# New tables of order, banks and engines for an attention and mixer kernel, with every ReLU on ScalarE

## The chip, the cores and the metric

The kernel runs on one core of a Trainium2 chip. The metric is the time of one execution in microseconds (us) on the device. A core has five engines that run side by side, each through its own instructions in a fixed order: TensorE (PE, matmuls into PSUM banks), VectorE (DVE), ScalarE (ACT), GpSimd (POOL) and SyncE (SP), which here issues all DMAs. An instruction starts when the one before it on its engine has begun to leave room and when the semaphores it waits for are set.

## The reference

Block-causal attention (8 batches, 8 heads, 576 positions, head width 64, blocks of 64), then a mixer over its output x (576 positions, 512 channels):

```
scores = scale * q @ k^T, masked by blocks;  attn = softmax(scores);  x = attn @ v
theta = x @ w_theta;  zr = x * cos(theta);  zi = x * sin(theta)
y = w_tok_r @ zr + w_tok_i @ zi          (over positions)
u = x + y
out = u + max(u @ w_ch, 0)               (w_ch over channels)
```

## The kernel before

Matmul operands are split into two float16 halves (a high part and the difference), and a product is taken as high*high + low*high + high*low, so each of the mixer's products is three matmuls. For the first three batches the scores are taken in float32 without a split.

The work is a list of 3404 parts. Per pair of heads: wide and narrow scores (`s1`, `s2`, and a small `sd`) into PSUM banks; per head the maxima of the score rows on VectorE (`m`, line 633), a bias from them (`mn`, L641, VectorE or GpSimd), the exponentials on ScalarE (`e`, L646), the cast to the high half (`high`, L431 or L433), the subtraction for the low half (`low`, L436), a transposing DMA (`turn`, tile `pt`), 45 small matmuls with v (`weighted`, L680), and the division (`normalise`, L692 to L698, tile `xn`). Per batch: x is split and turned (tiles `xp`, `xT`), theta is made (L816, L819), its turns taken off (L828 on ScalarE, L834 on VectorE), sines and cosines (L849, L851), products with x (L860, tiles `aa`, `rr`), their halves (`zh` by L431 or L433, `zl` by L436), the mix over positions (L884), x added back (L889, L893, tile `u`), halves of u (L423 to L427, L900), the channel products (L907), the ReLU (`relu`, L910 to L915), the last addition (L923) and the store. Eight batches overlap: the attention of a later batch runs beside the mixer of an earlier one. At the beginning the weights are loaded, brought to float32 (L471 to L485), scaled and split (L494 to L507) beside the attention of the first batch.

Three tables decide what the parts leave open. `ORDER` is the order in which all parts are written out; each engine runs its own parts in that order. `BANKS` gives each PSUM tile one of the eight banks, seen as `s` (banks 0 to 3) and `g` (4 to 7) in the rows. `PLACES` gives one letter to each part that may run on more than one engine (A ScalarE, D VectorE, P GpSimd). `emit` (L236) reads them:

```
        if parts[key].on:
            place[key] = next(places, parts[key].on[0])
```

The ReLU can be on ScalarE or VectorE:

```
            if on == "A":
                nc.scalar.activation(out=c, in_=c, func=AF.Relu, scale=self.scales["v"].unit)
            else:
                nc.vector.tensor_scalar(out=c, in0=c, scalar1=self.scales["v"].unit, scalar2=0.0, op0=ALU.mult, op1=ALU.max)
```

Of the kernel before, what the change touches and what calls it, by code (L numbers as in the profile page):

```python
# [37 lines left out]
    8, 9, 158, 10, 11, 160, 336, 335, 363, 364, 340, 339, 16, 17, 18, 19, 350, 341, 0, 1, 2, 3, 32, 33, 351, 334,  # L38
    361, 352, 34, 386, 24, 338, 337, 342, 25, 387, 372, 40, 41, 26, 27, 390, 392, 343, 12, 42, 35, 353, 162, 415,
    362, 365, 163, 4, 20, 414, 344, 43, 391, 56, 57, 48, 366, 373, 49, 58, 59, 374, 72, 375, 50, 51, 401, 367, 354,  # L40
    385, 164, 345, 346, 347, 44, 80, 36, 412, 413, 368, 73, 369, 74, 165, 28, 166, 64, 389, 104, 388, 393, 416, 96,
    88, 81, 355, 159, 161, 402, 52, 82, 60, 65, 97, 5, 105, 106, 13, 75, 376, 394, 403, 66, 21, 29, 89, 136, 137,
    138, 139, 348, 67, 37, 423, 424, 425, 167, 168, 169, 170, 417, 171, 45, 395, 53, 172, 76, 107, 120, 98, 99, 112,
    332, 333, 437, 396, 489, 83, 438, 349, 100, 404, 377, 405, 442, 441, 90, 370, 383, 418, 465, 84, 384, 61, 397,
    68, 69, 494, 91, 77, 466, 108, 356, 85, 92, 398, 93, 101, 141, 178, 176, 443, 357, 142, 436, 151, 474, 358, 426,
    30, 22, 359, 371, 452, 113, 143, 14, 6, 419, 114, 115, 420, 378, 440, 439, 434, 399, 121, 122, 444, 453, 379,
    463, 421, 464, 467, 445, 435, 446, 128, 15, 140, 144, 447, 540, 406, 468, 469, 454, 116, 46, 448, 470, 123, 180,
    86, 487, 427, 380, 475, 381, 31, 54, 471, 449, 490, 400, 476, 491, 360, 38, 407, 428, 514, 455, 382, 495, 496,
    408, 515, 409, 518, 410, 488, 497, 129, 493, 456, 517, 519, 130, 492, 422, 450, 457, 516, 477, 525, 429, 503,
    504, 498, 485, 505, 472, 430, 431, 478, 173, 94, 174, 152, 479, 432, 486, 131, 539, 568, 567, 526, 78, 527, 182,  # L50
    451, 506, 507, 544, 499, 543, 520, 1804, 458, 109, 538, 591, 145, 500, 1805, 411, 459, 545, 181, 508, 554, 460,
    461, 433, 541, 576, 501, 521, 528, 529, 522, 124, 70, 132, 542, 480, 566, 117, 546, 125, 133, 146, 577, 147,
    473, 481, 183, 184, 482, 39, 153, 185, 549, 483, 1807, 555, 186, 1808, 596, 556, 557, 530, 187, 509, 565, 569,
    7, 502, 188, 510, 558, 511, 512, 578, 547, 47, 579, 523, 531, 548, 550, 551, 462, 148, 580, 149, 118, 134, 126,
    189, 524, 532, 533, 484, 1806, 570, 571, 572, 534, 1810, 1811, 513, 1809, 589, 190, 150, 593, 592, 1837, 1838,
    154, 536, 587, 597, 598, 559, 535, 1813, 1812, 1823, 1814, 573, 552, 599, 1830, 23, 1831, 102, 1824, 617, 590,
    1839, 600, 616, 620, 1825, 62, 110, 537, 1832, 594, 1815, 595, 605, 588, 621, 622, 560, 606, 79, 574, 1816, 619,
    618, 71, 601, 111, 627, 607, 553, 608, 1826, 628, 1827, 561, 562, 563, 63, 1840, 1841, 1842, 1833, 609, 602,
    629, 1817, 1818, 1828, 1834, 1835, 1819, 581, 1829, 1844, 1845, 623, 1846, 1847, 1820, 1843, 1848, 575, 630,
    582, 1821, 1822, 1836, 177, 179, 610, 1849, 1850, 1851, 1852, 1860, 55, 1861, 603, 583, 638, 624, 87, 640, 103,  # L60
    584, 668, 644, 585, 667, 671, 642, 672, 625, 631, 1856, 1853, 673, 196, 641, 647, 643, 648, 649, 650, 95, 645,
    670, 646, 1864, 1854, 656, 1857, 1865, 611, 657, 604, 693, 651, 586, 194, 658, 669, 564, 1855, 678, 639, 612,
    652, 632, 1868, 1858, 698, 198, 613, 691, 614, 653, 615, 694, 1862, 692, 695, 1869, 679, 680, 659, 1859, 1870,
    654, 1866, 699, 197, 700, 701, 720, 633, 626, 634, 1908, 696, 1863, 1909, 697, 635, 1910, 1899, 1900, 1901, 660,
    1867, 661, 719, 1914, 689, 681, 690, 674, 119, 636, 199, 707, 1885, 708, 1889, 1871, 1872, 709, 721, 1911, 718,
    1902, 200, 682, 637, 1915, 1873, 675, 683, 722, 1916, 702, 703, 1912, 1881, 729, 676, 704, 705, 723, 710, 711,
    712, 1917, 1888, 655, 1880, 662, 2004, 1918, 1903, 1876, 195, 1893, 1894, 663, 1895, 1896, 664, 1907, 1919, 665,
    1892, 666, 2005, 2006, 1884, 1904, 1897, 1913, 744, 1898, 2007, 1877, 730, 731, 724, 2008, 201, 202, 203, 725,
    732, 733, 734, 684, 677, 726, 685, 1882, 1878, 743, 1879, 749, 686, 748, 687, 1886, 1890, 1874, 742, 1891, 1875,
    785, 727, 747, 745, 746, 688, 750, 751, 204, 205, 752, 706, 713, 714, 766, 715, 1944, 1945, 1883, 764, 753, 716,  # L70
    1946, 754, 755, 765, 206, 1887, 207, 1938, 767, 208, 155, 1939, 756, 156, 768, 769, 757, 135, 1940, 770, 1941,
    1947, 1948, 1942, 2010, 740, 1937, 209, 2009, 735, 1943, 771, 728, 772, 773, 781, 1949, 741, 736, 783, 737, 738,
    786, 758, 784, 789, 2023, 790, 2024, 788, 717, 826, 787, 739, 759, 791, 792, 806, 2037, 794, 1920, 1921, 795,
    796, 1905, 793, 2013, 807, 2030, 805, 808, 809, 2031, 2011, 2038, 831, 867, 797, 774, 2012, 2039, 2014, 760,
    761, 191, 2025, 192, 2032, 812, 813, 798, 127, 810, 1922, 2044, 2045, 782, 2046, 2015, 2047, 2048, 1950, 2033,
    2049, 775, 2026, 2027, 2028, 2034, 811, 2035, 157, 2040, 1906, 2041, 2042, 175, 2016, 2017, 2050, 2029, 2018,
    2019, 762, 825, 2020, 2021, 824, 1951, 2043, 2036, 799, 2022, 2051, 763, 212, 830, 829, 216, 849, 220, 2052,
    2061, 814, 815, 816, 828, 2053, 1929, 1930, 1931, 1932, 1933, 1934, 827, 776, 832, 777, 778, 833, 835, 836,
    1923, 1924, 846, 848, 1925, 1926, 847, 822, 779, 780, 1927, 800, 1952, 834, 823, 1928, 1935, 850, 1958, 1959,
    1994, 1936, 1976, 1977, 1978, 837, 2080, 1995, 1996, 801, 838, 839, 840, 1997, 853, 1953, 854, 851, 852, 193,  # L80
    1960, 1961, 1954, 802, 1979, 1970, 855, 1962, 2068, 2056, 2060, 2064, 803, 1980, 804, 2057, 817, 856, 857, 1998,
    1971, 1972, 1973, 2081, 818, 2058, 2059, 1981, 2062, 2085, 1955, 213, 2063, 1999, 819, 1963, 820, 872, 1974,
    1956, 865, 221, 863, 1957, 1975, 217, 866, 2000, 214, 888, 1964, 869, 1965, 1966, 871, 870, 1967, 1968, 868,
    873, 874, 875, 841, 876, 878, 2069, 2070, 1969, 2077, 864, 842, 218, 2054, 2089, 821, 1982, 877, 2055, 2092,
    1983, 2099, 2100, 1984, 1985, 222, 843, 887, 890, 2093, 889, 2094, 891, 2065, 844, 879, 2088, 845, 892, 2066,
# [1091 lines left out]
```

## Time and profile before

| what | us |
|---|---|
| time, median of 3 runs (lowest to highest) | 668.06 (667.66 to 668.56) |
| time of the profiled execution | 667.24 |
| its span, first to last instruction | 665.5 |
| TensorE busy (share of the span) | 611.8 (92%) |
| VectorE busy | 583.9 (88%) |
| ScalarE busy | 508.4 (76%) |
| GpSimd busy | 380.9 (57%) |
| mean granted clock of TensorE, share of full | 0.97 |

The span is the time from the first to the last instruction; the profiled execution took 1.7 us more than that. A busy TensorE is not one at its peak, since matmuls overlap. The durations of rows are those of single instructions; neighbours on an engine overlap a little, so that their sum is above the busy time.

### The profile page before, as it was taken

What the parts mean: (1) busy time and instruction counts of PE and PEld (TensorE: products, weight loads), DVE (VectorE), ACT (ScalarE), POOL (GpSimd) and SP (SyncE); (2) the same over time, 40 slices, a digit from 0 to 9 for tenths busy, and PEclk for the clock granted to TensorE, in tenths of its full rate; (3) what the DMA queues carried; (4) which work ended last, traced back from release to release, by engine and by line L of the source; (5) the groups of instructions that cost most, each with busy time, mean ns of one, the idle gap of its engine ahead of it and who ended that gap; (6) DMA issues with size and microseconds to landing.
All of it is one profiled execution on the core that took longest, in us unless ns stands there. A gap on an engine that the chain in (4) does not pass through costs nothing. (4 is left out here: it accounts for less than half of the span.)

```text
span 665.5 us, 18051 instructions
## 1 busy us (share of the span) xinstructions
PE 611.8 (92%) x7372; PEld 455.0 (68%) x7374; DVE 583.9 (88%) x1149; ACT 508.4 (76%) x777; POOL 380.9 (57%) x397
## 2 busy tenths in 40 slices
PE   4487697999999999999999998998899999999997
PEld 3255455876777588775788766785677578857775
DVE  4899989999999999998999899998998999745564
ACT  5978879776988898987998889887997988326011
POOL 3544656834453567555785829673597459752640
PEclk9577988999999999999999999999999999999999
DMA  9999999997889489989778897789789537950002
GB/s 360 364 252 210 211 179 240 233 191 151 214 203 204 98 203 197 199 161 208 191 180 164 152 218 165 184 163 195 196 188 206 107 70 138 173 99 1 19 37 89
DMA packets 268515, 116.58 MB, mean 175 GB/s; under 512 B 256016, under 2 KB 256016, under 8 KB 268432
## 3 DMA queue, kind: packets, MB, share of 16 engines
q1 hardware_dynamic: 268432, 115.43, 79.5%
q8 instruction: 57, 0.93, 0.6%
q14 instruction: 26, 0.21, 0.1%
HBM read 42.01 MB, written 9.44 MB: 77 GB/s over the span
## 5 line engine op out<-in xcount | busy, mean ns | idle before, releaser
L884 PEld LDWEIGHTS <-zh 128*128 128x128 f16 x1152 | 112.6, 98 | 30.9 <-issue 1.9
L680 PE MATMUL g<-v,pt 128*128 128x65 f16 x2880 | 102.3, 196 | 11.3 <-DMA pt<-p 5.1
L680 PEld LDWEIGHTS <-pt 128*128 128x128 f16 x2880 | 98.6, 99 | 20.0 <-issue 9.4
L884 PE MATMUL g<-wT_h,zh 128*128 128x288 f16 x369 | 105.8, 287 | 0.6 <-ACT t L646 0.6
L884 PE MATMUL g<-wT_h,zl 128*128 128x288 f16 x369 | 105.7, 287 | 0.1
L884 PE MATMUL g<-wT_l,zh 128*128 128x288 f16 x369 | 105.7, 287 | 0.0
L436 DVE TENSOR_TENSOR p<-t,p 128x1600 f16<-128x1600 f32 (+4 forms) x57 | 91.7, 1610 | 1.9 <-ACT p L431 1.8
L633 DVE TENSOR_REDUCE m<-s 128x1 f32<-128x576 f32 (+2 forms) x132 | 85.8, 671 | 4.3 <-PE s L596 4.2
L431 ACT CAST p<-t 128x1536 f16<-128x1536 f32 (+4 forms) x65 | 82.2, 1273 | 3.1 <-DMA pt<-p 2.1
L860 POOL TENSOR_TENSOR aa<-aa,xn 128x256 f32<-128x256 f32 (+1 forms) x69 | 53.8, 792 | 44.4 <-ACT aa L849 43.9
L436 POOL TENSOR_TENSOR p<-t,p 128x512 f16<-128x512 f32 (+4 forms) x23 | 53.8, 2345 | 35.8 <-ACT p L431 25.0
L816 PEld LDWEIGHTS <-xT 128*128 128x128 f16 x384 | 36.3, 98 | 45.7 <-issue 3.5
L884 PEld LDWEIGHTS <-zl 128*128 128x128 f16 x576 | 56.4, 98 | 15.4 <-issue 0.7
L646 ACT ACTIVATE t<-s,m,size 128x576 f32<-128x576 f32 (+1 forms) x80 | 59.3, 779 | 9.9 <-POOL m L641 6.4
L884 PE MATMUL s<-wT_h,zh 128*128 128x288 f16 x207 | 59.3, 287 | 0.0
L884 PE MATMUL s<-wT_l,zh 128*128 128x288 f16 x207 | 59.3, 287 | 0.0
L884 PE MATMUL s<-wT_h,zl 128*128 128x288 f16 x207 | 59.3, 286 | 0.0
L907 PEld LDWEIGHTS <-wch_h 128*128 128x128 f16 x512 | 48.2, 98 | 15.1 <-issue 2.9
L633 DVE TENSOR_REDUCE m<-g 128x1 f32<-128x320 f32 (+2 forms) x156 | 54.2, 371 | 4.2 <-PE g L596 4.0
L646 ACT ACTIVATE t<-g,m,size 128x320 f32<-128x320 f32 (+2 forms) x100 | 49.4, 533 | 8.5 <-POOL m L641 7.6
L436 POOL TENSOR_TENSOR zl<-aa,zh 128x512 f16<-128x512 f32 (+1 forms) x38 | 44.6, 1177 | 10.1 <-DVE zh L433 5.4
L907 PE MATMUL g<-uh,wch_h 128*128 128x288 f16 x172 | 49.4, 287 | 1.0 <-DVE xT L923 0.7
(190 smaller groups left out, 1625.2 us busy)
## 6 DMA issues: line engine op xcount, KB each, us to landing
rv<-in_v SPq DMA_DIRECT2D x16, 768.0 KB, 5.7
rq<-in_q SPq DMA_DIRECT2D x16, 640.0 KB, 5.2
rk<-in_k SPq DMA_DIRECT2D x16, 576.0 KB, 5.2
out<-xT SPq DMA_DIRECT2D x32, 288.0 KB, 3.2
w_raw<-in_w_tok SPq DMA_DIRECT2D x5, 576.0 KB, 5.5
pt<-in_w_tok SPq DMA_DIRECT2D x4, 576.0 KB, 7.5
w_raw<-in_w_theta SPq DMA_DIRECT2D x4, 512.0 KB, 6.8
w_raw<-in_w_ch SPq DMA_DIRECT2D x4, 512.0 KB, 4.4
```

What stands on the lines that cost most here:

```text
L431: nc.scalar.copy(out=out, in_=x)
L436: engine_of(on).tensor_tensor(out=out, in0=x, in1=y, op=ALU.subtract)
L633: nc.vector.tensor_reduce(out=self.m[:, i:i + 1], in_=self.scores_of(i), axis=AX.X, op=ALU.max)
L646: nc.scalar.activation(out=t_parts[self.hh][:, to:to + n], in_=self.scores_of(i), func=AF.Exp, scale=self.scales()[0], bias=self.m[:, NI + ...
L680: nc.tensor.matmul(o[:, i, :], lhsT=source[:, block, :], rhs=vv[:, slot, hh, :], start=first, stop=last)
L816: nc.tensor.matmul(g, lhsT=xT[:, xx + i, :], rhs=ww[:, dt, :], start=first, stop=last)
L860: engine_of(on).tensor_tensor(out=cd, in0=cd, in1=self.xns[dt][:, i0:i0 + ni, :], op=ALU.mult)
L884: nc.tensor.matmul(g, lhsT=zz[:, kk, cols], rhs=ww[:, kk, ts], start=(n == 0 and kk == k0 and nn == 0), stop=n == 4 and kk == k0 + ni - 1 ...
L907: nc.tensor.matmul(g[:, 0:HS], lhsT=ww[:, dt, e * P:(e + 1) * P], rhs=uu[:, dt, th * HS:(th + 1) * HS], start=dt == 0 and n == 0, stop=dt ...
```

## The change

Only the three tables change; no function does. All 64 letters for the ReLUs of the channel products are now A (before 38 were A and 26 D). The other letters, the order and the banks are new as well.

```diff
 ORDER = [
-    8, 9, 158, 10, 11, 160, 336, 335, 363, 364, 340, 339, 16, 17, 18, 19, 350, 341, 0, 1, 2, 3, 32, 33, 351, 334,
+    8, 9, 158, 160, 335, 10, 11, 0, 1, 16, 17, 2, 56, 340, 364, 363, 372, 373, 374, 336, 339, 57, 40, 3, 350, 58,
...
 PLACES = (
...
-    "PADPDDAPADPDADDAAAA"
+    "PADDADDPDPPAAAAAAAA"
 )
```

On VectorE, where the channel products of the first batch are finished (L915 is the ReLU, L923 the last addition into tile `xT`, the others belong to heads), before:

```order
L436 TENSOR_TENSOR p_100<-t_98,p_100 128x1536
L915 TENSOR_SCALAR s_109<-s_109,size 128x288
L692 TENSOR_SCALAR r<-g_114 128x5
L923 SCALAR_TENSOR_TENSOR xT<-u_2179,size,s_109 128x288
L923 SCALAR_TENSOR_TENSOR xT<-u_1980,size,s_109 128x288
L694 RECIPROCAL r<-r 128x5
L923 SCALAR_TENSOR_TENSOR xT<-u_1731,size,g_112 128x288
```

and now:

```order
L436 TENSOR_TENSOR p_100<-t_98,p_100 128x1536
L923 SCALAR_TENSOR_TENSOR xT<-u_1705,size,s_109 128x288
L923 SCALAR_TENSOR_TENSOR xT<-u_2008,size,s_109 128x288
L923 SCALAR_TENSOR_TENSOR xT<-u_1705,size,g_113 128x288
L692 TENSOR_SCALAR r<-g_114 128x5
L694 RECIPROCAL r<-r 128x5
L923 SCALAR_TENSOR_TENSOR xT<-u_2237,size,g_111 128x288
```

The ReLU row is gone from VectorE, and three additions stand together there. On ScalarE at the same place (L913 is the ReLU, L431 the cast of a head's probabilities, L778 the sums of magnitudes of a later batch), before:

```order
L431 CAST p_100<-t_98 128x1536
L913 ACTIVATE g_112<-g_112,size 128x288
L913 ACTIVATE s_109<-s_109,size 128x288
L431 CAST zh<-rr 128x512
L431 CAST zh<-aa 128x512
L778 ACTIVATE junk,size<-rq 128x1280
L913 ACTIVATE g_111<-g_111,size 128x288
L913 ACTIVATE g_113<-g_113,size 128x288
```

and now:

```order
L431 CAST p_100<-t_98 128x1536
L913 ACTIVATE s_109<-s_109,size 128x288 x2
L913 ACTIVATE g_113<-g_113,size 128x288
L913 ACTIVATE g_112<-g_112,size 128x288
L913 ACTIVATE g_111<-g_111,size 128x288
L778 ACTIVATE junk,size<-rk 128x1152
```

Five ReLUs stand in a row on ScalarE, and the two casts of z are elsewhere. On GpSimd near the start, in the first two heads (L433 casts and L436 subtractions of probabilities `p`, L479 and L641 small work on weights and biases, L368 a diagonal for the scale of v), before:

```order
L433 CAST p_99<-t_97 128x512
L479 TENSOR_SCALAR w_raw<-w_raw 128x576
L433 CAST p_100<-t_98 128x512
L479 TENSOR_SCALAR w_raw<-w_raw 128x576
L641 TENSOR_SCALAR m<-m 128x2
L433 CAST p_100<-t_98 128x1024
L436 TENSOR_TENSOR p_100<-t_98,p_100 128x1024
L479 TENSOR_SCALAR w_raw<-w_raw 128x576
```

and now:

```order
L433 CAST p_99<-t_97 128x512
L436 TENSOR_TENSOR p_99<-t_97,p_99 128x512
L436 TENSOR_TENSOR p_100<-t_98,p_100 128x512
L641 TENSOR_SCALAR m<-m 128x3
L641 TENSOR_SCALAR m<-m 128x2
L479 TENSOR_SCALAR w_raw<-w_raw 128x512
L436 TENSOR_TENSOR p_99<-t_97,p_99 128x1088
L368 TENSOR_SCALAR diag<-ident_r,size 128x128
```

Three subtractions of the first two heads are now on GpSimd ahead of the diagonal, where one stood there before. On PE at the very start (L589 narrow scores, L617 the first block's score), before:

```order
L617 MATMUL g_114<-rk,rq 128x64
L589 MATMUL g_111<-rk,rq 128x320
L589 MATMUL g_113<-rk,rq 128x320
L589 MATMUL g_111<-rk,rq 128x128
L589 MATMUL g_113<-rk,rq 128x128
```

and now:

```order
L589 MATMUL g_113<-rk,rq 128x320
L589 MATMUL s_109<-rk,rq 128x320
L589 MATMUL g_113<-rk,rq 128x128
L589 MATMUL s_109<-rk,rq 128x128
L589 MATMUL g_113<-rk,rq 128x64
```

The narrow scores of one head of pair 0 now stand in bank s_109, which wide scores need next; before, both heads' were in g banks.

## Rows read from the trace of the kernel before

**Rows 1.** Busy time by stretch: us, then PE, PEld, DVE, ACT, POOL busy, clock, DMA.

```profile
0.00:103.00 103.00, 70.91 (x728) 47.32 (x731) 87.67 (x188) 82.87 (x140) 51.38 (x75) 0.83 1.03 264
103.00:120.00 17.00, 12.78 (x191) 10.32 (x188) 16.68 (x35) 16.80 (x25) 10.46 (x15) 0.90 1.12 240
120.00:300.00 180.00, 177.46 (x2226) 134.64 (x2224) 171.79 (x344) 152.47 (x234) 98.69 (x99) 1.00 0.89 184
300.00:440.00 140.00, 135.67 (x1805) 101.69 (x1804) 130.92 (x259) 120.88 (x179) 94.73 (x87) 1.00 0.85 182
440.00:545.00 105.00, 98.78 (x1289) 71.19 (x1285) 98.40 (x187) 93.76 (x137) 61.98 (x60) 1.00 0.78 160
545.00:661.40 116.40, 116.21 (x1153) 89.84 (x1150) 77.95 (x141) 41.14 (x65) 63.70 (x63) 1.00 0.40 84
661.40:665.50 4.10, 0.00 (x0) 0.00 (x0) 0.52 (x1) 0.47 (x1) 0.00 (x0) 0.76 0.18 72
```

**Rows 2.** Waits of PE, 0 to 120 us: who for whom, us in total, times, longest.

```profile
PE s L589 <- ACT t L646: 5.8, 4, 3.7
...
PE g L680 <- DMA pt<-p: 3.6, 4, 1.8
```

**Rows 3.** Waits of PE, 120 to 545 us.

```profile
PE g L680 <- DVE xn L698: 2.0, 2, 1.4
PE s L816 <- ACT t L646: 1.7, 1, 1.7
PE s L907 <- ACT t L646: 1.6, 1, 1.6
PE g L680 <- DMA pt<-p: 1.6, 4, 1.0
PE g L374 <- POOL diag L368: 1.0, 1, 1.0
PE g L589 <- DVE u L893: 0.9, 1, 0.9
PE g L617 <- DVE xn L698: 0.9, 2, 0.5
PE g L907 <- DVE xT L923: 0.7, 1, 0.7
```

**Rows 4.** Timeline, first uses of theta on VectorE and ScalarE: start, us, what.

```profile
99.37 0.74 DVE L834 SCALAR_TENSOR_TENSOR rr<-g,size,aa 128x512 f32<-128x512 f32 x1
97.87 1.26 ACT L828 ACTIVATE aa<-g,size 128x512 int32<-128x512 f32 x2
```

**Rows 5.** VectorE, groups with shapes apart: busy us, mean ns, idle before.

```profile
L436 DVE TENSOR_TENSOR p<-t,p 128x1088 f16<-128x1088 f32 x7 | 12.3, 1755 | 0.0
L915 DVE TENSOR_SCALAR g<-g,size 128x288 f32<-128x288 f32 x16 | 8.2, 515 | 0.2 <-PE g L907 0.2
L436 DVE TENSOR_TENSOR p<-t,p 128x512 f16<-128x512 f32 x8 | 6.4, 794 | 0.0
L915 DVE TENSOR_SCALAR s<-s,size 128x288 f32<-128x288 f32 x10 | 5.2, 520 | 1.6 <-PE s L907 1.5
```

**Rows 6.** ScalarE's ReLUs on g banks, groups with shapes apart.

```profile
L913 ACT ACTIVATE g<-g,size 128x288 f32<-128x288 f32 x27 | 12.7, 474 | 26.0 <-PE g L907 26.0
```

**Rows 7.** GpSimd's subtractions of probabilities, groups with shapes apart.

```profile
L436 POOL TENSOR_TENSOR p<-t,p 128x512 f16<-128x512 f32 x8 | 9.4, 1176 | 6.6 <-ACT p L431 5.1 <-DVE m L641 0.8 <-POOL m L641 0.6
L436 POOL TENSOR_TENSOR p<-t,p 128x1088 f16<-128x1088 f32 x1 | 2.8, 2779 | 0.0
```

**Rows 8.** Timeline, two subtractions on VectorE and GpSimd's beside them.

```profile
24.95 2.48 POOL L436 TENSOR_TENSOR p<-t,p 128x1024 f16<-128x1024 f32 x1
25.48 3.10 DVE L436 TENSOR_TENSOR p<-t,p 128x1088 f16<-128x1088 f32 x1
56.20 1.28 DVE L436 TENSOR_TENSOR p<-t,p 128x1088 f16<-128x1088 f32 x1
56.88 2.60 POOL L436 TENSOR_TENSOR p<-t,p 128x1024 f16<-128x1024 f32 x1 [1.33 <-ACT p L431]
```

More of the change, by code (lines that the diff above doesn't have):

```diff
@@ L37 @@
 ORDER = [
[176 rows of a table removed]
[176 rows of a table added]
 ]
 BANKS = (
-    "6640455415101234601234501235401235401236501230101236401235601234601236501236401236501234601234501235401234501234"
-    "5012356012354012364012346012346012345012356012356012364012356012364012346012354012365012356246515041550565440441"
-    "5460560214666650466150524616666244541656064530665500455604466101503640144155446541520126505646466544456100451342"
-    "31315450463621054620463501434154206"
+    "4556164551001236001234501234601235601235401231001236501236401235401234601235601235601235601234501235401235401235"
@@ L220 @@
+    "4012346012354012346012346012345012354012356012356012346012356012365012346012364012365012365246551650445606454041"
+    "6540151630666461566050425316646355451406665420444500465601466501605440544155446405425450164156455646416040451634"
+    "52245163452601620132435450513216524"
 )
 PLACES = (
-    "ADAAAAADPPAPAADPAAPAAPAAPAAADAADPAAAPAAADPPAPAAPAAPADDDPPDDPPPPDPDADPADDADPDDPDADPAPDAPDDPDPADPAPDAPDAPAPADPAPPA"
-    "DPPDADAPPAPPADPPDDPADPADPADPAPAPADPADDADPAPAPADDADPDADDDDPDADDADADADDADAADPADDAPAAPPADDAPAAAPADDADPPAPADPADAPADA"
@@ L224 @@
-    "PPADAAAPDDPAPAAADADPAPPDPDADDADAAAPAPPADADPDPDPADAAPDADPPDPAAPADDADAAPDADDADAAPPADPPDAAPPADPAPAAAPADDADAAAPADDDP"
-    "AAAPDDDAPAAPPAPPAPPPPPADPADDDAPADAPADDAAPDDDPPAPPPAPPDADPPDPDDAPDPADDDAPPPADPPAPPADPPDDAAAAAADADADADAPDPAAAAAPDP"
-    "PPDAPPPAPPPAPPPDDDPAPDDPDDPAPPPADPPPPPADAPAPAADDDAADAPDADAPDDDAAAAPPAPDPAPDPADDDAPPPPPDDAPPPADDPAPPDAPPPPPPPPAPP"
-    "PDDAAAADAAPPPDAPDDADADDPPAPPDAPPDPPDPAPPPAPPDAPPPAPDDPPPPADPDAPPAPPDPDADAAADDADAPAPAPAPAADDDPPADPPPPPPAPDPAPPPAP"
-    "DPAPPPAPDPAPPDADPPAPPPDADPPADDDDADADAPADAPAPAADDDPDPPPPAPPPPPDPAPPPPPPPAPDDADPPAPPPAPDPAPDADPDDPAAAADAAAAPDADDPA"
@@ L229 @@
-    "DAAADAPPADPDADPPADPDADPDPPPPPDPDPPPDDPPPPPPPPPPAPADAPDADDAADADPDDPPPADDDADADPPDDDDPPPAPPPPDDPPPPPPDPPPPDDDPPDAPP"
-    "PADPDDAPADPDADDAAAA"
+    "DAAPDAPAAADAAAAAAPDAPDAAPAAAAAPAAPAAPAAPAADAAPADAAAAPDPPPPDDDDAPPDAPPAPDDDDAPPDADPPPDAPPPPADADPAPPAPPPPAPADPPDDP"
+    "DDPPPDAPPAPPADPPDDPADPAPPADPAPADADPADDADPAPAPADDADPPAPPPDPPADPADAPADPADAADPADDAPAAPPADPAPAAADADPADPPADADPADAPADA"
+    "PPADAAADDDPAPAAADADDAPPPPPADDADAAPPAPDADAAPDPDPADAAPDADPPDAPAPADPADAAPDADPAPAAAPADPPDAAPPADPAPAAAPADPADAAAPADPDP"
@@ new lines @@
+    "AAPPDDPAPAAPPAPPAPPPPPADDADPDAPADAPADDAAPPPDDDAPPPAPDPADPPAPPDAPPPAPDDAPPDAPPPPPPADPPDDPAAAAAAAAADADAPPDAADADPPP"
+    "PDDPPPDPPPPAPPDAPDPADPPPPPPADPPADPPAPDADAPAPDAAAAAAAAAPAPAPDDDAAAAPDPPDPAPDDDPPDAPDPPDPPAPDPAPDPAPDDADPDPPPAPPDP"
+    "PDAAAAAAAAAPPPPPDDAAAADPDADPDAPPPPPDDPPPDPPPDAPPPAPDPAPPPAPDPPPPAPAPADAAAAAAAAAAPAPAPPPDAAADDPAPPPPDPPAPPPAPPPAD"
+    "PPAPPDAPDPAPDDADPDPPPAPAPADAAAAAAAAAAPADPPAPAADADPDPPPPPPPPPPDDADPPPDPPAPDDPDDDAPPDAPDPAPDAPPDDDAAAAAAAAAPDAPAPA"
+    "DAAADAPPAPPPAPDPAPPDAPPPPPPDPPPPAPPPPPPDPPDDAPDADAPDDAAAAAAAAAAPPDAPPDDDDADPDAPDPADDDAPDPPDDPADPPDDDDAPDPPPPPDPP"
```

350 rows, old and new, of the table ORDER are left out of this document.

## The prediction

> **What bounds the kernel now.** I read the stages first [rows 1]: busy time of each engine in seven stretches. TensorE is the busiest engine, and the matmuls do not change, so the question is only where it stands idle. Stretch length less PE busy time gives 32.1 us idle up to 103 us, 4.2 up to 120, then 2.5, 4.3 and 6.2 in the three stretches from 120 to 545, 0.2 up to 661.4, and 4.1 in the tail, where one ReLU, one addition and a store are left. That is 36.3 us at the start, 13.0 in the middle and 4.3 at the end.
>
> In the same rows VectorE is the next one: from 120 to 545 us it is busy 171.8 + 130.9 + 98.4 = 401.1 of 425 us (94%), ScalarE 367.1 (86%), GpSimd 255.4 (60%). In 545 to 661.4 VectorE has slack and PE runs without a gap. So the middle is a stretch where PE and VectorE are nearly full together, and each lateness of VectorE shows as a small PE stall.
>
> Next the waits of PE. At the start [rows 2] they stand behind ScalarE's exponentials, which free the score banks, and the transposing DMA of the probabilities (pt). In the middle [rows 3] eight rows make 10.4 of the 13.0 us: VectorE ends 2.0 + 0.9 + 0.9 + 0.7 = 4.5 of them, ScalarE 3.3, the DMA of pt 1.6, GpSimd's diagonal 1.0.
>
> Then what fills the start. The first VectorE instruction that takes a theta product (L834) begins at 99.37 us, and ScalarE's first one (L828) at 97.87 [rows 4]. Ahead of them stand, by counting each form in the order of the engine and multiplying with its mean duration, 96.7 us of VectorE work and 90.2 us of ScalarE work. VectorE is full up to there, ScalarE nearly so. GpSimd has 51.4 us of work in 103 [rows 1].
>
> **The change, part by part.** Every part is still there, and PE has the same 14,210 rows of order before and after, with other banks and neighbours. What moves is VectorE, ScalarE and GpSimd work, and I counted each form over each engine's whole order.
>
> ReLUs. VectorE loses all 26 of them: 16 on g banks at 0.515 us and 10 on s banks at 0.520 are 13.4 us [rows 5]. ScalarE gets them at 0.474 each [rows 6], 12.3 us more, 64 in place of 38. In the tail nothing changes: the last ReLU stands on ScalarE in both.
>
> The splits. The subtraction of the second half (L436) on the probabilities goes from 57 to 49 on VectorE and from 23 to 31 on GpSimd. The two forms that move most at the start are 128x512, 0.794 us on VectorE and 1.176 on GpSimd, and 128x1088, 1.755 against 2.779 [rows 5, 7]. With those of x and z L436 falls by 16.2 us on VectorE and grows by 25.2 on GpSimd. Counted the same way, casts take 4.3 more from VectorE and smaller groups 3.3; six more products with x in each of two forms (L860) and two more sums (L889) give back 8.3; the rest is within 2. Net: VectorE 30.9 us less, ScalarE 12.1 more, GpSimd 25.8 more.
>
> The start. Ahead of the same first theta instruction VectorE now has 89.6 us (7.1 less), ScalarE 89.5 (0.7 less). GpSimd has 57.8 in place of 49.5 ahead of its first product with x, with fifteen subtractions of probabilities there in place of ten. If VectorE alone sets the start it is 7.1 us shorter; if ScalarE does, 0.7. I take 3.0, nearer to ScalarE, because it was within 8 us of full as well and its load stays. The first PE rows also change (a narrow score goes into an s bank, and the wide score of pair 0 then waits for two exponentials): ScalarE has 22 parts ahead of the exponential that frees the banks of the next wide score, before it had 21, so I cost this at nothing. Its cover is ScalarE's early queue; if that is late, the 3.65 us kind of wait that is part of the 5.8 in [rows 2] grows with it.
>
> The middle. Of VectorE's 30.9 us less, 7.1 are gone at the start and about 1 falls behind 545, so 401.1 becomes about 378; ScalarE rises by some 10 to 377. Of 425 us both are then at 89%, in place of one at 94%. I take 9.0 of the 13.0 us of PE idle as gone: the 4.5 that VectorE ends, the diagonal's 1.0 (GpSimd makes it from a maximum that VectorE reduces), and somewhat under half of the 7.5 behind exponentials, DMAs and the small rows that are left out, since those wait for maxima and differences that VectorE makes. The bounds are none and 13.0. What is late next is ScalarE: its ReLUs now free the channel banks, and they queue behind exponentials and casts.
>
> The price on GpSimd. Two subtractions of one form, 128x1088 on VectorE, show what a neighbour costs [rows 8]: the one that began at 25.48, 0.53 us after a GpSimd subtraction, took 3.10 us; the one at 56.20 began before GpSimd's, at 56.88, and took 1.28. So a GpSimd subtraction can hold a VectorE one back by 1.8 us. GpSimd gets 14 more rows of L436 in all; at most that is 14 x 1.8 = 25 us of VectorE time, at least nothing (the VectorE one begins first, as at 56.20). The durations of rows 5 are means over both cases, so most of it is in the numbers already, and I take nothing more; 25 is kept for the slow rival.
>
> The Trainium skill (SBUF — State Buffer, "Who interferes with whom") says that a VectorE instruction with two SBUF inputs and a GpSimd instruction that reads SBUF exclude each other for the whole instruction, whoever is first. By that rule each of GpSimd's added microseconds can shut VectorE's subtractions out, which speaks against this change; the pair in rows 8 agrees with it, and a sum by it alone would leave VectorE only 30.9 - 25 = 6 us lighter.
>
> The sum: the profiled execution took 667.24 us, of which the span is 665.5 and 1.7 lies around it. 667.24 - 3.0 - 9.0 = 655.2. The median of the three runs, 668.06, is 0.8 above the profiled one, so I say 656.0.
>
> **The rivals.**
> VectorE was behind everything. It speaks for this that it is full in every stretch until 545 us; against it, that ScalarE ends 3.3 us of the mid waits and had 90.2 us of work at the start. Then 7.1 + 13.0 go: 667.24 - 20.1 + 0.8 = 648.
>
> ScalarE takes VectorE's place. For it: its load ahead of the first theta product is level, it has 120.9 of 140 and 93.8 of 105 us busy in the late middle, and a ReLU that waits for its turn holds a bank that a score or mix wants. Against it: 89% is not 94%. Then only 0.7 goes: 667.24 - 0.7 + 0.8 = 667.3.
>
> GpSimd's early subtractions make it slower. The place is the first 100 us, where heads come one after another, each through cast, subtraction, transposing DMA and products. GpSimd does five more of the subtractions there. Each can hold a VectorE one for 1.8 us, 9.0 together, against the 7.1 that VectorE saves; and the head's own chain is longer by 0.38 for four forms of 128x512 and by 1.02 for two of 128x1088, less 0.9 for one 128x1024 that goes away (2.48 us in [rows 8], at the ratio of 128x1088), 2.7 in all. That is 9.0 - 7.1 + 2.7 = 4.6 us later at the start. In the middle the locked-out 25 us take back VectorE's relief and the 13.0 stay: 667.24 + 4.6 + 0.8 = 672.6. It decides from the point where the five no longer fit into GpSimd's idle half of the first 103 us. Against it: that half is 51.6 us. The rule of the skill named above is the same mechanism.
>
> **How the numbers follow.** Chances: 0.45 for the forecast (656, its own range 651 to 661), 0.20 for the big gain (648), 0.15 for ScalarE in VectorE's place (667.3), 0.20 for the slow start (672.6). About 0.2%, 1.3 us, is what a measurement can tell from no change. Faster takes the first two and a little of the third: 0.67. Within 0.2% is most of the third and some of the fourth: 0.13. Slower: 0.20. The range 645 to 670 holds the first three and the milder part of the last; about 0.2 is left out.
>
> **What would show it.** Right: in the stretches of [rows 1], PE's idle time up to 120 us is about 33 and from 120 to 545 about 4; VectorE is at or below 90% there and ScalarE near 89%; the waits of PE named after xn, u and xT shrink. The big gain: under 30 at the start. ScalarE's place: mid waits of PE of the old size, most of them ended by ScalarE's exponentials, ReLUs or the additions behind them. The slow start: PE waits for pt longer than the 3.6 us of [rows 2], GpSimd's subtractions as the releaser, and VectorE's subtractions at 3 us more often. I am wrong if PE's idle time at the start grows, or if the mid idle time stays while VectorE is lighter.

## The result and the profile after

The changed kernel takes 677.11 us (median of 4 runs, 673.96 to 680.48) against 668.31 for the kernel before (4 runs, 667.66 to 668.71). The ratio is 1.0137, 95% interval 1.0111 to 1.0164: slower by 1.4%, where 656 was forecast. Its profiled execution took 676.17 us, its span is 674.4, 8.9 longer than before.

VectorE and ScalarE moved about as counted: VectorE's busy time fell from 583.9 to 557.4 us (26.5, counted 30.9), ScalarE's rose from 508.4 to 519.7 (11.3, counted 12.1). GpSimd's rose only from 380.9 to 390.5, by 9.6 where 25.8 were counted: its subtractions (L436) grew by 23.9, but its products with x (L860) fell by 10.5 and its L427 by 6.7. TensorE's waiting did not fall. These are the seven stretches again, the columns as in [rows 1]:

```profile
0.00:103.00 103.00, 71.53 (x752) 49.43 (x754) 85.47 (x184) 81.35 (x141) 57.07 (x80) 0.82 1.02 266
103.00:120.00 17.00, 12.45 (x133) 9.43 (x134) 14.82 (x32) 14.99 (x21) 9.14 (x13) 0.80 0.96 222
120.00:300.00 180.00, 176.44 (x2242) 134.59 (x2239) 158.84 (x327) 150.89 (x232) 111.74 (x116) 0.99 0.88 183
300.00:440.00 140.00, 133.65 (x1745) 100.16 (x1745) 123.36 (x242) 126.35 (x191) 85.81 (x83) 1.00 0.85 183
440.00:545.00 105.00, 98.64 (x1269) 70.92 (x1267) 93.79 (x184) 93.83 (x139) 63.41 (x63) 1.00 0.78 161
545.00:661.40 116.40, 112.43 (x1181) 87.44 (x1176) 76.99 (x136) 48.59 (x78) 63.31 (x59) 1.00 0.36 74
661.40:674.40 13.00, 8.91 (x73) 6.87 (x71) 4.15 (x9) 3.71 (x8) 0.00 (x0) 0.93 0.29 113
```

Stretch less PE busy gives PE's idle time. Up to 120 us it is 36.0, before 36.3: the start gained nothing. From 120 to 545 it is 3.6 + 6.3 + 6.4 = 16.3, before 13.0. From 545 to 661.4 it is 4.0, before 0.2. VectorE is lighter in the middle about as forecast (376.0 of 425 us, 88%), and TensorE waits more.

The waits of PE from 120 us to the end, which answer to [rows 3], say for what (us in total, times, longest):

```profile
PE s L589 <- DVE xT L923: 5.8, 3, 2.7
PE g L907 <- DVE ul L900: 2.8, 2, 2.6
PE g L680 <- DVE xn L698: 2.5, 3, 1.0
PE g L907 <- DVE xT L923: 1.6, 2, 1.2
PE s L374 <- POOL diag L368: 1.5, 1, 1.5
PE s L907 <- ACT t L646: 1.5, 1, 1.5
PE g L680 <- DMA pt<-p: 1.3, 4, 0.7
PE g L884 <- DVE xT L923: 1.0, 1, 1.0
```

The addition behind the ReLU (L923, tile xT) ends 8.4 us in these rows, all of them before 545 us, where [rows 3] had 0.7. All other waits of PE from 120 to 545 us, taken together, fell from 11.8 to 7.4 us. So there was a relief of 4.4 us, and the additions took back 7.7 (rows of 0.2 us counted in). How much of the 4.4 is the lighter VectorE, and how much is that the other engines catch up while PE stalls, is not separated.

In the queue of VectorE before that addition stands the reason. What VectorE's L923 waited for over the whole span, before:

```profile
DVE xT L923 <- ACT s L913: 1.5, 2, 1.0
DVE xT L923 <- ACT g L913: 1.5, 2, 1.0
```

and after:

```profile
DVE xT L923 <- ACT g L913: 20.6, 16, 3.1
DVE xT L923 <- ACT s L913: 14.0, 9, 4.0
```

VectorE waits 34.6 us for ReLUs in place of 3.0. Before, all of that lies behind 657 us. After, 14.3 us lie behind 545 us, where VectorE has slack, and the rest in the middle (120 to 545 us):

```profile
DVE xT L923 <- ACT g L913: 13.1, 10, 1.8
DVE xT L923 <- ACT s L913: 7.2, 3, 4.0
```

That is 20.3 us where before there was no such wait, and VectorE was made lighter there by 25.1 (401.1 to 376.0): most of the relief has turned into waiting. One such wait, at 270 us (timeline of the changed kernel):

```profile
263.74 0.29 PE L907 MATMUL s<-uh,wch_l 128*128 128x288 f16 x1
264.46 0.71 ACT L431 CAST xp<-xn 128x640 f16<-128x640 f32 x1
265.07 1.45 ACT L646 ACTIVATE t<-s,m,size 128x576 f32<-128x576 f32 x2
266.41 1.16 ACT L778 ACTIVATE junk<-rk 128x1152 uint8<-128x1152 f32 x1
267.56 1.47 ACT L431 CAST p<-t 128x1536 f16<-128x1536 f32 x1
268.92 0.48 ACT L913 ACTIVATE s<-s,size 128x288 f32<-128x288 f32 x1
269.44 0.52 DVE L923 SCALAR_TENSOR_TENSOR xT<-u,size,s 128x288 f32<-128x288 f32 x1 [3.98 <-ACT s L913]
270.00 0.66 PE L589 MATMUL s<-kh,qh 64*128 64x512 f16 x4 [2.67 <-DVE xT L923]
```

The channel products in the s banks have all ended by 264.03 (263.74 + 0.29). ScalarE has four other pieces of work in front of this ReLU and gets to it 4.89 us after that; the ReLU takes 0.48, the addition 0.52, and only then is the bank free for the next score. VectorE stood 3.98 us with nothing to do, TensorE 2.67. The Trainium skill (PSUM — Partial Sum Buffer, "Engine vs sequencer instructions") says that the queues of ScalarE and VectorE are strict first in, first out; these rows agree, a ready ReLU passes nobody and nobody passes the waiting addition. This stall costs more than itself, as the clock column of windows of 2 us shows:

```profile
270.00:272.00 2.00, 2.00 (x18) 1.02 (x19) 1.33 (x4) 1.97 (x3) 1.97 (x3) 0.50 0.43 175
272.00:274.00 2.00, 2.00 (x33) 1.44 (x30) 1.14 (x2) 0.35 (x2) 2.00 (x2) 0.73 0.41 156
```

Both stood at 1.00 before. At 0.50 (the level of 1.2 GHz) and 0.73 some 1.0 + 0.5 us more are lost, by an estimate from these two rows. Not every stall does this: in the same profile a wait of 2.4 us at 400 us and one of 2.57 at 558 us left the clock at 1.00. Over the whole span PE is idle 6.7 us longer and busy 2.2 us longer (614.0 against 611.8), together the 8.9.

At the start the waits answer to [rows 2] (PE, 0 to 120 us):

```profile
PE g L589 <- DMA rk<-in_k: 7.8, 1, 7.8
PE s L589 <- ACT t L646: 7.6, 1, 7.6
PE g L617 <- DVE xn L698: 3.4, 2, 2.2
```

The wait for ScalarE's exponentials has grown from 5.8 to 7.6 and is now one piece. And there is one more loss, at 557 us:

```profile
557.07 3.43 POOL L436 TENSOR_TENSOR p<-t,p 128x1600 f16<-128x1600 f32 x1
557.47 3.65 DVE L900 SCALAR_TENSOR_TENSOR ul<-u,u_scales,uh 128x576 f16<-128x576 f32 x1
...
561.17 0.28 PE L907 MATMUL g<-ul,wch_h 128*128 128x288 f16 x1 [2.57 <-DVE ul L900]
```

A VectorE difference of 0.96 us mean (32 of them) began 0.40 us behind a GpSimd subtraction and took 3.65, the kind of pair that [rows 8] showed. VectorE's subtractions (two forms of them) and ScalarE's ReLUs, which answer to [rows 5, 6], are these after:

```profile
L436 DVE TENSOR_TENSOR zl<-rr,zh 128x512 f16<-128x512 f32 x9 | 7.4, 819 | 0.0
L436 DVE TENSOR_TENSOR p<-t,p 128x1088 f16<-128x1088 f32 x5 | 7.0, 1394 | 2.0 <-ACT p L431 2.0
```

```profile
L913 ACT ACTIVATE g<-g,size 128x288 f32<-128x288 f32 x41 | 19.0, 474 | 8.6 <-PE g L907 8.5
...
L913 ACT ACTIVATE s<-s,size 128x288 f32<-128x288 f32 x23 | 10.8, 474 | 27.9 <-PE s L907 24.8 <-PE s L884 1.7 <-DVE xT L923 1.2
```

A ReLU costs ScalarE the forecast 474 ns. VectorE's subtractions have become shorter in some forms (1394 for 1755 ns) and longer in others (819 for 696). All 80 of them together take 105.6 us, and they would take 105.6 at the means of before: in sum the added GpSimd work did not stretch them.

### The profile page after: what moved, and what is told of

Read it like the earlier page. It is cut to its first block, busy times and chain, and to the rows that moved or that the text cites. A ratio compares the mean times of both kernels' runs of the same rounds, so it can differ in the third digit from the quotient of the medians.

```text
span 674.4 us, 18049 instructions
## 1 busy us (share of the span) xinstructions
PE 614.0 (91%) x7372; PEld 458.8 (68%) x7374; DVE 557.4 (83%) x1108; ACT 519.7 (77%) x804; POOL 390.5 (58%) x411
## 4 chain that ended last, share of the span: by engine, by line
PE 62%; DVE 12%; ACT 11%; DMA 8%; issue 3%; POOL 1%; SPq 1%; DVEq 0%; ACTq 0%; POOLq 0%
PE g L884 17%; PE s L884 8%; PE g L680 7%; PE s L589 6%; PE g L816 5%; DMA pt<-p 5%; PE g L907 5%; PE s L816 4%; ACT t L646 4%; PE s L907 4%; PE g L589 3%; DVE m L633 3%; DMA rk<-in_k 2%; DVE p L436 2%; ACT aa L849 1%
## 5 line engine op out<-in xcount | busy, mean ns | idle before, releaser
L884 PE MATMUL g<-wT_h,zh 128*128 128x288 f16 x405 | 116.1, 287 | 1.1 <-DVE xT L923 1.0
L884 PE MATMUL g<-wT_l,zh 128*128 128x288 f16 x405 | 116.0, 286 | 0.0
L884 PE MATMUL g<-wT_h,zl 128*128 128x288 f16 x405 | 116.0, 286 | 0.0
L680 PE MATMUL g<-v,pt 128*128 128x65 f16 x2880 | 104.8, 197 | 12.1 <-DVE xn L698 5.1
L436 POOL TENSOR_TENSOR p<-t,p 128x512 f16<-128x512 f32 (+4 forms) x31 | 70.2, 2268 | 44.0 <-ACT p L431 26.8
L633 DVE TENSOR_REDUCE m<-s 128x1 f32<-128x576 f32 (+3 forms) x134 | 86.3, 668 | 9.3 <-PE s L596 9.0
L431 ACT CAST p<-t 128x1600 f16<-128x1600 f32 (+4 forms) x62 | 79.8, 1291 | 7.4 <-DMA pt<-p 6.4
L436 DVE TENSOR_TENSOR p<-t,p 128x1600 f16<-128x1600 f32 (+4 forms) x49 | 80.6, 1647 | 4.5 <-ACT p L431 3.7
L860 POOL TENSOR_TENSOR aa<-aa,xn 128x256 f32<-128x256 f32 (+1 forms) x63 | 50.2, 807 | 27.6 <-ACT aa L849 25.1
L646 ACT ACTIVATE t<-g,m,size 128x192 f32<-128x192 f32 (+2 forms) x100 | 49.4, 533 | 6.8 <-DVE m L641 3.4
L436 POOL TENSOR_TENSOR zl<-aa,zh 128x512 f16<-128x512 f32 (+1 forms) x38 | 46.4, 1225 | 13.6 <-PE g L617 6.9
L907 PE MATMUL g<-ul,wch_h 128*128 128x288 f16 x164 | 46.9, 286 | 2.8 <-DVE ul L900 2.8
L884 PE MATMUL s<-wT_l,zh 128*128 128x288 f16 x171 | 49.0, 286 | 0.0
```

The lines of the kernel that those rows point to most:

```text
L431: nc.scalar.copy(out=out, in_=x)
L436: engine_of(on).tensor_tensor(out=out, in0=x, in1=y, op=ALU.subtract)
L633: nc.vector.tensor_reduce(out=self.m[:, i:i + 1], in_=self.scores_of(i), axis=AX.X, op=ALU.max)
L646: nc.scalar.activation(out=t_parts[self.hh][:, to:to + n], in_=self.scores_of(i), func=AF.Exp, scale=self.scales()[0], bias=self.m[:, NI + ...
L680: nc.tensor.matmul(o[:, i, :], lhsT=source[:, block, :], rhs=vv[:, slot, hh, :], start=first, stop=last)
L860: engine_of(on).tensor_tensor(out=cd, in0=cd, in1=self.xns[dt][:, i0:i0 + ni, :], op=ALU.mult)
```

## The experiments

The theory: a ReLU on ScalarE waits in its queue, the addition on VectorE waits for the ReLU, and the bank and PE wait for both. First rival: GpSimd's added subtractions hold VectorE back. Second: a ReLU on ScalarE costs the time wherever it stands. All kernels compute the whole result. Each was timed in five rounds. They ran on three chips (e1 to e4, e5 to e7, e8 and e9), so kernels are compared by their ratios to the kernel before on the same chip. The diffs of `PLACES` show one of the lines that differ.

**e1_old_relus.** The changed kernel with the letters of the 64 ReLUs as before (26 on VectorE).

```
...
-    "PPAPPDAPDPAPDDADPDPPPAPAPADAAAAAAAAAAPADPPAPAADADPDPPPPPPPPPPDDADPPPDPPAPDDPDDDAPPDAPDPAPDAPPDDDAAAAAAAAAPDAPAPA"
+    "PPAPPDAPDPAPDDADPDPPPAPAPADADDDDADADAPADPPAPAADADPDPPPPPPPPPPDDADPPPDPPAPDDPDDDAPPDAPDPAPDAPPDDDAAADAAAAPDAPAPA"
...
```

> The changed kernel with the 26 ReLUs that were on VectorE before put back there; order, banks and all other letters stay new. Theory 1 (on ScalarE a ReLU stands in a queue behind exponentials, casts and sines; the addition on VectorE and then PE wait for it): VectorE's waits for ScalarE's ReLUs fall from 34.6 us to under 15, PE's waits named xT from 8.6 to under 3, time about 668 (664 to 671). Rival 2 (GpSimd's added subtractions hold VectorE back): the time stays at 674 to 679, since those are untouched and VectorE gets 13.4 us more to do.

Measured: 675.9 us, ratio 1.0125 (1.0099 to 1.0151). Next to nothing came back, and the expectation missed. The old letters do not fit the new order: L923 still waits for 12 ReLUs on ScalarE (10 in the row below, 2 on s banks), and ReLUs now on VectorE wait for PE at the head of its queue. VectorE's waits:

```profile
DVE xT L923 <- ACT g L913: 12.3, 10, 2.7
DVE g L915 <- PE g L907: 3.7, 3, 1.7
DVE s L915 <- PE s L907: 2.9, 3, 1.7
```

The loss moved: PE waits 2.6 us in one piece for a ReLU on VectorE (L915), where it waited for L923. Against e3_late_relus_dve below, which has fewer ReLUs on VectorE, PE is idle 3.0 us longer from 120 to 545 us and 3.2 longer behind 545, where it waits for VectorE (zl 1.2, xn 0.9, xT 0.9). Which ReLU stands where counts, not how many.

**e2_relus_alone.** The kernel before, its 26 ReLUs of VectorE on ScalarE, nothing else changed.

```
...
-    "DPAPPPAPDPAPPDADPPAPPPDADPPADDDDADADAPADAPAPAADDDPDPPPPAPPPPPDPAPPPPPPPAPDDADPPAPPPAPDPAPDADPDDPAAAADAAAAPDADDPA"
+    "DPAPPPAPDPAPPDADPPAPPPDADPPAAAAAAAAAAPADAPAPAADDDPDPPPPAPPPPPDPAPPPPPPPAPDDADPPAPPPAPDPAPDADPDDPAAAAAAAAAPDADDPA"
...
```

> The kernel before with its 26 VectorE ReLUs put on ScalarE and nothing else changed. Theory 1: VectorE's waits for ScalarE's ReLUs rise from 3.0 us to over 15, time 672 to 679. Rival 2: 667 to 669, or a little faster, since VectorE is 13.4 us lighter and GpSimd is as before.

Measured: 678.72 us, ratio 1.0153 (1.0128 to 1.0179), as slow as the whole change. VectorE's waits and then PE's:

```profile
DVE xT L923 <- ACT g L913: 13.9, 15, 2.5
DVE xT L923 <- ACT s L913: 9.3, 8, 4.4
```

```profile
PE s L589 <- DVE xT L923: 5.3, 3, 4.1
```

The ReLUs alone make a loss of this size, in another order and with other splits, by the same chain of waits.

**e3_late_relus_dve.** The changed kernel with 15 ReLUs on VectorE: those of its first seven batches for which L923 waited 0.9 us or more.

```
...
-    "PPAPPDAPDPAPDDADPDPPPAPAPADAAAAAAAAAAPADPPAPAADADPDPPPPPPPPPPDDADPPPDPPAPDDPDDDAPPDAPDPAPDAPPDDDAAAAAAAAAPDAPAPA"
+    "PPAPPDAPDPAPDDADPDPPPAPAPADADADDAADAAPADPPAPAADADPDPPPPPPPPPPDDADPPPDPPAPDDPDDDAPPDAPDPAPDAPPDDDAADAAAADPDAPAPA"
...
```

> The changed kernel with only those 15 ReLUs on VectorE whose addition had made VectorE idle for 0.9 us or more (batches 0 to 6). Theory 1: nearly the whole loss comes back with 7.7 us of VectorE work: 664 to 670, PE's waits named xT under 3 us. Rival 2: 674 to 679.

Measured: 668.27 us (12 runs), ratio 1.0005 (0.9986 to 1.0023). The whole loss is gone. VectorE's waits and PE's:

```profile
DVE xT L923 <- ACT g L913: 6.2, 8, 1.5
DVE xT L923 <- ACT s L913: 5.7, 6, 2.3
```

```profile
PE s L589 <- DVE xT L923: 0.7, 1, 0.7
```

**e4_moved_lows_dve.** The changed kernel with ten subtractions of probabilities back from GpSimd to VectorE, most of them of the first heads.

```
...
-    "DAAPDAPAAADAAAAAAPDAPDAAPAAAAAPAAPAAPAAPAADAAPADAAAAPDPPPPDDDDAPPDAPPAPDDDDAPPDADPPPDAPPPPADADPAPPAPPPPAPADPPDDP"
+    "DAAPDAPAAADAAAAAAPDAPDAAPAAAAAPAAPAAPAAPAADAAPADAAAAPDDPPDDDDDADPDADPADDDDDADPDADPPPDAPPPPADADPAPPAPPPPAPADPPDDP"
...
```

> The changed kernel with the 10 subtractions of probabilities that moved from VectorE to GpSimd (nine of them in the first 13 heads, one in head 18 or 49) put back on VectorE; the ReLUs stay on ScalarE. Theory 1: 673 to 679, since the mid-run waits stay. Rival 2: the loss comes back at the start and in the middle, 666 to 670.

Measured: 683.48 us, ratio 1.0237 (1.0210 to 1.0265): 6.4 us above the changed kernel, and L923 waits for ReLUs as long as there (20.7 + 13.1). The first stretch of its windows:

```profile
0.00:103.00 103.00, 70.68 (x746) 48.25 (x747) 88.13 (x190) 81.10 (x140) 44.41 (x73) 0.80 1.01 265
```

GpSimd has 12.7 us less there, VectorE 2.7 more, and PE is idle longer, not shorter (32.3 for 31.5). From 120 to 545 us PE is idle 19.9 us in place of 16.3, and its waits behind xn (VectorE) are 4.4 there in place of 1.5. The first rival, which was my slow case, falls for these ten: on GpSimd they help this order. The added subtractions of x and z on GpSimd were not put back in any run.

**e5_hoisted.** All ReLUs stay on ScalarE; five of them are written earlier in `ORDER`, by 1 to 13 places, to where their product is done and ahead of what stood before them there. (The expectation says four; of batch 2 two were moved.) The one of the stall at 270 us goes ahead of three parts:

```
- ... place 1411: ('relu', 1, 3, 0)
+ ... place 1408: ('relu', 1, 3, 0)
```

> The changed kernel with all ReLUs still on ScalarE, but four of them moved forward in the order past the exponentials, casts and sums that stood between the end of their channel product and them (batch 0, 1, 2 and 4; the one of batch 1 that cost PE 2.67 us passes one exponential, one sum and one cast). The others stand behind sines or directly behind their product and can't be moved so. Theory 1, that the place in ScalarE's queue is what costs: the wait at 270 us goes, with the slow clock behind it some 4 us, time 671 to 674. Rival 3, that a ReLU on ScalarE costs whatever its place (its own 0.47 us, one more hand-over between engines): 676 to 678, as the changed kernel.

Measured: 673.56 us, ratio 1.0097 (1.0070 to 1.0125); the changed kernel's was 1.0137. At the place of the stall (its line numbers are 5 lower):

```profile
265.44 0.47 ACT L908 ACTIVATE s<-s,size 128x288 f32<-128x288 f32 x1
...
265.94 0.52 DVE L918 SCALAR_TENSOR_TENSOR xT<-u,size,s 128x288 f32<-128x288 f32 x1 [0.85 <-ACT s L908]
...
266.90 0.42 PE L584 MATMUL s<-kh,qh 64*128 64x512 f16 x4
```

The ReLU starts at 265.44 in place of 268.92 and the score follows without a wait. It is the place in the queue that costs, not the engine: the second rival falls at this place, and over the whole kernel five moves give back about a third. The intervals of 1.0137 and 1.0097 overlap, so that third is measured roughly. The other long stall behind L923, 2.4 us, is still there: its ReLU was not among the five.

**e6_six_relus.** As e3_late_relus_dve with six of the 15, those at the stalls of PE.

```
...
-    "PPAPPDAPDPAPDDADPDPPPAPAPADAAAAAAAAAAPADPPAPAADADPDPPPPPPPPPPDDADPPPDPPAPDDPDDDAPPDAPDPAPDAPPDDDAAAAAAAAAPDAPAPA"
+    "PPAPPDAPDPAPDDADPDPPPAPAPADADADDAADAAPADPPAPAADADPDPPPPPPPPPPDDADPPPDPPAPDDPDDDAPPDAPDPAPDAPPDDDAAAAAAAAAPDAPAPA"
...
```

> The changed kernel with only six ReLUs on VectorE: those whose lateness stood behind PE's waits at 270, 403, 481, 495 and 499 us. Theory 1: most of the 8.8 us that fifteen gave back, time 669 to 673. Rival 3 (each ReLU on ScalarE costs about the same): six of fifteen give back 3.5 us, 673.5.

Measured: 670.88 us (12 runs), ratio 1.0041 (1.0022 to 1.0061). Six ReLUs bring back two thirds of the loss. PE's waits behind L923 are as small as with 15 (0.7 + 0.7 + 0.5 + 0.2), though VectorE still waits 24.4 us for ReLUs: most of that waiting was harmless. By the ratios the other nine are worth a further 0.4%; the two intervals just meet (1.0022 and 1.0023), so it may be nothing, and these two profiles show no cause.

**e7_one_low_more.** As e3_late_relus_dve, and the subtraction of head 61 on VectorE, to free the ul at 557 us.

```
...
-    "AAPPDDPAPAAPPAPPAPPPPPADDADPDAPADAPADDAAPPPDDDAPPPAPDPADPPAPPDAPPPAPDDAPPDAPPPPPPADPPDDPAAAAAAAAADADAPPDAADADPPP"
+    "AAPPDDPAPAAPPAPPADPPPPADDADPDAPADAPADDAAPPPDDDAPPPAPDPADPPAPPDAPPPAPDDAPPDAPPPPPPADPPDDPAADAAAAAADADAPPDAADADPPP"
...
```

> The fifteen ReLUs on VectorE, and one subtraction of probabilities (head 61, 128x1600) moved from GpSimd to VectorE as well. GpSimd's one ran 557.07 to 560.50 in the changed kernel and VectorE's subtraction for u beside it took 3.65 us in place of 0.81, which PE waited 2.57 us for. If GpSimd's subtraction held it back: that instruction takes about 0.8 to 1.3 us, PE's wait for ul is gone, and the time is 1 to 2.5 us below the 668.3 of the fifteen alone. If it was something else: no change, 668 to 669, or 1 more for VectorE's 1.84 us.

Measured: 668.51 us, ratio 1.0002 (0.9981 to 1.0024). I had taken the wrong part: the subtraction beside ul is that of head 60. PE waits for ul as long as before (2.6 us), and ul takes 3.66 us beside a GpSimd subtraction of 3.44. So moving a subtraction that does not stand beside ul changes nothing, which makes this run a control for the next.

**e8_relus_and_low.** As e3_late_relus_dve, and the subtraction of head 60 on VectorE.

```
...
-    "AAPPDDPAPAAPPAPPAPPPPPADDADPDAPADAPADDAAPPPDDDAPPPAPDPADPPAPPDAPPPAPDDAPPDAPPPPPPADPPDDPAAAAAAAAADADAPPDAADADPPP"
+    "AAPPDDPAPAAPPADPAPPPPPADDADPDAPADAPADDAAPPPDDDAPPPAPDPADPPAPPDAPPPAPDDAPPDAPPPPPPADPPDDPAADAAAAAADADAPPDAADADPPP"
...
```

> The changed kernel with the 15 late ReLUs on VectorE and the one subtraction that stood beside the 3.65 us ul at 557 us (that of head 60) on VectorE instead of GpSimd. If the shared port is what stretched ul (3.65 us beside GpSimd's 3.43 us against 0.80 in its free form), ul falls to 0.8 to 1.3 us, TensorE's wait of 2.57 us for it goes, and the time is 1.5 to 3 us under that with the 15 ReLUs alone (668.3): 665.5 to 667. The rival: ul is late because VectorE's queue ahead of it is late, and the subtraction there makes it later by its 1.3 us: ul stays behind its product, TensorE waits as long, 668 to 670.

Measured: 666.34 us (12 runs, 663.54 to 669.64), ratio 0.9975 (0.9953 to 0.9997). It is faster than both kernels, than the one before by little: the interval ends just under 1. The ul and the subtraction behind it, both on VectorE:

```profile
549.88 0.90 DVE L900 SCALAR_TENSOR_TENSOR ul<-u,u_scales,uh 128x576 f16<-128x576 f32 x1
550.70 0.95 DVE L860 TENSOR_TENSOR aa<-aa,xn 128x256 f32<-128x256 f32 x1
551.57 1.81 DVE L436 TENSOR_TENSOR p<-t,p 128x1600 f16<-128x1600 f32 x1
...
554.75 0.31 PE L589 MATMUL g<-kh,qh 64*128 64x320 f16 x2 [1.65 <-DVE xT L923]
```

ul takes 0.90 us and the wait for it is gone; a smaller wait, 1.65 us behind the addition that VectorE now reaches later, stands in its place. The Trainium skill (SBUF — State Buffer, "Who interferes with whom") has the pair of VectorE and GpSimd shut each other out for a whole instruction; 3.65 us beside GpSimd's 3.43 and 0.90 without it agree.

**e9_start.** As e8_relus_and_low, and among places 40 to 74 of `ORDER` the 14 steps that decode weights stand behind the steps of the attention.

```
-    25, 26, 362, 20, 414, 353, 354, 48, 33, 376, 104, 49, 164, 43, 338, ...
+    362, 414, 353, 354, 376, 164, 338, 361, 365, 366, 337, 355, 342, ...
```

> As the run before it, and in ORDER, among the 35 steps that follow the first wide scores (places 40 to 74), the 14 steps that decode weights are put behind the steps of the attention, in their own order. It asks where the 3.0 us forecast for the start went: in the changed kernel TensorE waits 7.60 us at 15 to 22.95 us for the exponentials that read its score, and between the maxima on VectorE stand 1.20 us of decoding (16.33 us), between the exponentials on ScalarE 1.46 us (19.66 us). If the order of the start is what keeps that wait, it falls by 2 to 2.7 us and so does the time (663.5 to 665). If the weights are what the start waits for, the decoding that is put off comes back as a wait for weights (the rows of the theta products) and the time is the same within 1 us or longer.

Measured: 670.63 us (12 runs), ratio 1.0027 (1.0010 to 1.0044), 4.3 us above e8_relus_and_low. PE's score waits fell from 7.8 us in e8_relus_and_low to 5.5, and a new wait came (timeline of PE, line numbers 5 lower):

```profile
21.78 4.10 PE L584 MATMUL s<-rk,rq 64*128 64x512 f32 x16 [5.49 <-ACT t L641]
...
33.72 0.27 PE L369 MATMUL g<-diag,ones 128*128 128x128 bf16 x1 [4.36 <-POOL diag L363]
```

The order of the early steps does set the score wait, but what is put off is in the way within 12 us: decoding steps now stand on VectorE in front of a cast of probabilities, which starts at 29.70 us in place of 26.31. GpSimd's subtraction waits for that cast, and the diagonal (L363) stands behind the subtraction. The first use of theta on VectorE comes at 103.85 us in place of 99.94, and that 3.9 us is most of the loss. It is not the wait for weights that the expectation named.

## Why the prediction was wrong

**The middle: -9.0 us forecast, +3.3 measured.** This is the step that failed, by the sign that the prediction had named: the mid idle time stays while VectorE is lighter. VectorE came down to 88% (forecast 89%), so the size of the relief was right; the inference from a lighter VectorE to shorter waits was not. Other waits did shrink, by 4.4 us, but the waits for the additions behind the ReLUs, a term that I had put at nothing, grew by 7.7. The sentence on what is late next, ScalarE, whose ReLUs "queue behind exponentials and casts", named the mechanism and put no price on it. Its price is the place of each ReLU in an in-order queue: 4.89 us of other work in front of 0.48. Taking 26 ReLUs off VectorE saved it 13.4 us and, by e2_relus_alone, made it wait 23.2 us for them in the order of before, where it had waited 3.0. The share of busy time (89% each) that I weighed the rival by cannot show this.

**ScalarE in VectorE's place: forecast 667.3, chance 0.15.** The mechanism was this one, down to the additions behind the ReLUs as the releasers of PE; the size was off, since I ended it at no gain. I had bounded the middle by "none and 13.0", gain only. A hand-over between two in-order engines can add idle time, and not only leave it: e2_relus_alone has 18.6 us in the middle.

**The start: -3.0 forecast, -0.3 measured.** VectorE was not full there: the 96.7 us counted ahead of theta add up means of the whole run, while it was busy 84.2 of 99.4 us. Now it is busy 81.4 up to its first theta, 2.8 less and not 7.1, and that bought nothing. The first use of theta on VectorE is at 98.94 us (99.37 in [rows 4]; 98.5 to 99.9 in the six experiments with this start), ScalarE's at 97.88 (97.87). That ScalarE's level load and the score wait (7.6 for 5.8) set it is argued from the rows; no run separates them. The score wait, whose change I cost at nothing, grew as the sentence on its cover said it could. e9_start shows that it hangs on the order, though not that it can be had for free.

**GpSimd: forecast 672.6 as the slow rival.** Its time was nearest of all, by luck, since its mechanism was wrong: PE's wait for pt in the first 120 us, its sign, fell from 3.6 to 2.1 us, and e4_moved_lows_dve put ten of the subtractions back and lost 6.4 us. The 25.8 us more of GpSimd work that I had counted were 9.6. That VectorE and GpSimd shut each other out counted at one place, 557 us, which I had not looked at because PE had no wait there before; e3_late_relus_dve and e8_relus_and_low put it at 0.3%, with intervals that overlap.

**After 545 us: nothing forecast, +3.8 measured.** PE's cover there, 0.2 us idle before, went: 2.57 us behind ul and 1.0 behind xn. I had treated a stretch without waits as safe. What is left of the 8.9 us is PE itself, busy 2.2 us longer, which I had also put at nothing; some 1.5 of that is the slow clock behind the stall at 270 us.

**What the rest is worth.** With the late ReLUs back on VectorE the changed tables are level with before, and with ul freed 0.25% faster, just clear of no change. Of the 12 us forecast for all splits and the order, about 1.7 are there. In e8_relus_and_low VectorE is busy 389.8 us in the middle, 11.3 less than before, and PE is idle 10.7 us there, in place of 13.0. The largest waits left there are for exponentials (2.3), the diagonal (1.4), xn and pt (1.3 each). Which part of the tables brings the 1.7 is not separated.

## What to carry to other kernels

A short operation that frees a PSUM bank belongs on the engine that reaches it first after its product ends; count what stands ahead of it in that engine's order, in us, before counting what it takes. When work leaves a busy engine, look for the instruction on that engine that consumes the moved result: if it stands next in line, the saved time can turn into a wait for the other engine. And give a hand-over a bound on the losing side too, as large as the work in front of it.

## What was not expected of the hardware

A stall of PE of 2.67 us was followed by a granted clock of 0.50 in the next 2 us and 0.73 in the 2 after, which by the estimate above added 1.5 us to it. Equal stalls need not do that. The wait for ul, 2.6 us long in seven of the profiles, was followed by a clock near 0.50 in four of them (e1, e3, e4, e6) and left it at 1.00 in the changed kernel, e5 and e7.

One VectorE difference beside one GpSimd subtraction took 3.65 us in place of 0.90 and cost PE 2.57, more than any other single wait after 120 us but that at 270.
